# Weight transfers and later scores held to the written order, |w| of the later weights on VectorE, the gate's middle tap and edges on ACT and GpSimd: one core, attention, gated MLP and convolution

## The chip, the cores and the metric

The kernel runs on one core of one Trainium2 chip. The metric is the device time of one execution in microseconds. The kernel before takes 615.66 us, the median of three runs (614.83 to 617.19).

## The reference

Four batches of 576 rows, 8 heads of 64, width 512. All inputs and outputs are float32, except that the kernel gets the four large weights as 64-bit words and narrows them itself.

```python
# attention, causal window of 128 rows, a bias by distance
s = q @ k.T / 8 + bias
p = softmax(where(mask, s, -1e9));  x = p @ v
# first layer: a gated MLP whose gate mixes the rows
h = gelu(x @ w_in);  u, v = split(h)
v = (v - mean) / sqrt(var + 1e-6) * g_ln
x = x + (u * (w_sg @ v + b_sg)) @ w_out
# second layer: 3-tap convolution along the rows as a gate
h = relu(x @ w_in2)
c = cw[0]*h[t-1] + cw[1]*h[t] + cw[2]*h[t+1]
out = (h * sigmoid(c)) @ w_out2
```

## The kernel before, in words

Float32 products are made of three products of a high and a low part, so each operand is split into "hi" (a rounding copy) and "lo" (a subtraction) ahead of TensorE. In the trace `psv`, `psu`, `pss` and `pso` are the PSUM tiles of the first layer's four products (steps V, U, G and W), `psg` that of the second layer (g2, the step D, makes h and the gate; g3, the step F, makes the output), `sc`, `pT` and `o` the scores, the transposed weights and the output of the attention. q and k are loaded by steps L, V tiles by M, scores are C, their exponentials E, their norm N.

Batch 0's attention stands at the start. Then batch b's V, U, G and W are laid between the attention of batch b+1, for three rounds, while the sixteen pieces of each of the second layer's weights are narrowed and written back to a scratch in DRAM (`w2d`, two transfers for each piece, hi and lo). Stage 2 (from about 332 us) makes batch 3's V, U, G and W, and loads w_in2 back into SBUF (`w<-w2d`, 8 transfers of 512 KB); stage 3 runs D and F of the four batches.

A weight piece is narrowed by `narrowed` (L246): a transfer into a staging tile, |w| (L255 on ACT or L257 on VectorE, chosen by booked costs), a clamp (L259), three operations on bits (L260 to L262). For w_in (pieces i0.0 to i1.3, 512 KB each, five staging buffers) and w_out, `split` then makes hi and lo. For the second layer, `w2_piece` (L298) writes hi on GpSimd over the staging tile itself (L303), lo over the |w| tile, and sends both to DRAM; there are two staging buffers, so the next-but-one piece's transfer waits for that write to land.

`_steps` writes out the order of the steps by hand. The instructions are then ordered by the framework's scheduler; `tc.keep_in_program_order(ins)` pins an instruction behind the one that was traced before it on the same engine. Before the change only the |w| on ACT and the clamp are pinned. All transfers of these stages are issued from SP's queue, in order. The choice of an engine (`ON`, a list per operation) goes by booked costs.

In g2 the middle tap is `scaled(cc, ..., ON["tap"])` (its operation is L198), the outer taps are L645 and L646 on VectorE, the last 64 or first 64 columns of h times its gate are the "edge", split into `gr` hi (L181) and lo (L187).

## Time and profile before

| | |
|---|---|
| median of three runs | 615.66 us |
| profiled execution | 614.43 us, its span 612.4 us |
| mean granted TensorE clock | 0.975 of full speed |
| TensorE busy (PE) | 562.5 us, 92% of the span |
| VectorE (DVE) / ACT / GpSimd (POOL) | 399.1 / 244.7 / 256.2 us |

The page gives each engine's busy time. PE is the engine to follow: what the kernel can save is its idle time, some 50 us in all, and the time in which its clock was granted at less than full speed. A busy share says little of the others. DVE's 65% is made of stretches in which it is full and others in which it waits, and the same holds for SP's queue, whose transfers start in the order in which they are issued.

### The profile page before, as it was taken

To read this page: it belongs to the slowest core of one execution; us is meant where nothing else is said; L and a number is where in the kernel's file an instruction comes from. 1 tells how busy PE (TensorE), PEld (TensorE's weight loads), DVE (VectorE), ACT (ScalarE), POOL (GpSimd) and SP (SyncE) were. 2 spreads that over 40 slices of the span, in tenths; PEclk is the share of its full clock that TensorE was granted. 3 is DMA by queue.
4 is the path that set the end of the run, shared out by engine and by line. 5 is a ranking of instruction groups with operands and counts; after the bars stand their busy time and mean duration, and the time that the engine had idled before them with its cause. 6 is when DMAs were issued, how large, how long until landed. Compare 5 with 4: busy or idle time off the path is not lost.

```text
span 612.4 us, 10380 instructions
## 1 busy us (share of the span) xinstructions
PE 562.5 (92%) x3704; PEld 480.4 (78%) x3704; DVE 399.1 (65%) x981; ACT 244.7 (40%) x626; POOL 256.2 (42%) x403
## 2 busy tenths in 40 slices
PE   6499959799998999999999997996899999999998
PEld 3366649588778888779798897886789898998887
DVE  3877957454585885586875855759996666556600
ACT  4764107863026744127733211115445333334311
POOL 0763655962142741245542634425664223322310
PEclk9799969899999899999999999997999999999999
DMA  8733402141324144424235847662200100000011
GB/s 303 278 119 102 144 2 89 40 137 33 105 100 129 45 156 128 134 58 125 66 110 152 313 136 227 206 222 78 78 17 35 55 17 18 36 18 17 18 51 52
DMA packets 44851, 63.55 MB, mean 104 GB/s; under 512 B 4352, under 2 KB 27392, under 8 KB 44800
## 3 DMA queue, kind: packets, MB, share of 16 engines
q1 hardware_dynamic: 44656, 62.60, 31.5%
q8 instruction: 29, 0.48, 0.3%
q10 hardware_dynamic: 144, 0.29, 0.1%
q14 instruction: 22, 0.18, 0.1%
HBM read 45.05 MB, written 17.83 MB: 103 GB/s over the span
## 4 chain that ended last, share of the span: by engine, by line
PE 56%; DVE 17%; DMA 12%; POOL 5%; issue 4%; ACT 4%; SPq 0%; POOLq 0%; DVEq 0%; ACTq 0%
PE psg L168 26%; PE pso L168 6%; PE o L168 6%; PE sc L168 4%; PE psv L168 4%; PE pss L168 4%; DMA w<-in_w_in_dram 4%; PE pT L402 3%; DMA w<-in_w_out_dram 3%; DVE t L360 3%; DMA w2d<-w 3%; ACT t L142 2%; PE psu L168 2%; DVE wa L261 1%; DVE wa L259 1%
## 5 line engine op out<-in xcount | busy, mean ns | idle before, releaser
L168 PE MATMUL psg<-x2g,w 128*128 128x288 f32 x768 | 108.3, 297 | 0.1
L168 PEld LDWEIGHTS psg<-x2g,w 128*128 128x128 f32 x768 | 105.8, 190 | 2.1 <-ACT hb L641 0.3
L168 PE MATMUL psg<-wout,gh 128*128 128x512 f32 (+1 forms) x272 | 82.4, 387 | 8.0 <-ACT gh L177 8.0
L142 ACT ACTIVATE t<-t,mx 128x256 f32<-128x256 f32 (+1 forms) x144 | 67.2, 469 | 23.2 <-DVE mx L360 23.1
L168 PE MATMUL pss<-wsg,vn 128*128 128x256 f32 (+1 forms) x448 | 66.4, 304 | 7.0 <-DVE t L529 7.0
L168 PEld LDWEIGHTS pss<-wsg,vn 128*128 128x128 f32 x448 | 61.9, 194 | 8.7 <-DVE t L529 8.1
L168 PE MATMUL sc<-k,q 64*128 64x256 f32 (+2 forms) x320 | 53.7, 408 | 11.8 <-DMA q<-in_q_dram 6.3
L168 PEld LDWEIGHTS psg<-wout,gh 128*128 128x128 f32 x272 | 49.8, 190 | 18.8 <-ACT gh L177 8.9
L168 PE MATMUL psu<-xh,win 128*128 128x256 f32 (+1 forms) x256 | 54.9, 307 | 8.7 <-POOL win L181 5.9
L360 DVE CUSTOM_DVE_ANT_0 t<-sc,tab 128x256 f32<-128x256 f32 (+2 forms) x144 | 47.8, 379 | 17.3 <-PE sc L168 17.2
L168 PE MATMUL pso<-gh,wo 128*128 128x256 f32 (+1 forms) x256 | 55.0, 308 | 4.1 <-DVE t L529 1.6
L198 POOL TENSOR_SCALAR t<-t,r 128x256 f32<-128x256 f32 (+2 forms) x105 | 51.3, 506 | 14.0 <-DVE r L387 6.7
L181 POOL TENSOR_SCALAR gr<-gg 128x64 fp32r<-128x64 f32 x30 | 16.4, 547 | 94.8 <-DVE gg L187 94.8
L168 PEld LDWEIGHTS sc<-k,q 64*128 64x128 f32 (+1 forms) x320 | 30.2, 198 | 32.4 <-issue 13.5
L168 PE MATMUL psg<-wout,gl 128*128 128x512 f32 (+1 forms) x136 | 52.4, 385 | 1.3 <-POOL gl L187 1.3
L168 PEld LDWEIGHTS psu<-xh,win 128*128 128x128 f32 x256 | 42.7, 196 | 11.5 <-POOL win L181 6.4
L168 PE MATMUL psv<-win,xh 128*128 128x512 f32 (+1 forms) x160 | 49.9, 397 | 0.0
L168 PEld LDWEIGHTS pso<-gh,wo 128*128 128x128 f32 x256 | 40.6, 190 | 9.0 <-DVE x L187 2.1
L187 POOL TENSOR_TENSOR gl<-gg,gh 128x512 fp32r<-128x512 f32 x32 | 43.9, 1375 | 8.2 <-ACT gh L177 8.2
L168 PE MATMUL o<-ph,V 128*64 128x128 f32 (+2 forms) x448 | 41.3, 301 | 3.1 <-ACT ph L177 2.9
L198 DVE TENSOR_SCALAR cc<-hb,cw 128x576 f32<-128x576 f32 x30 | 20.3, 680 | 30.3 <-ACT hb L641 30.3
L181 POOL TENSOR_SCALAR w<-wa 128x256 fp32r<-128x256 f32 x32 | 13.7, 428 | 62.4 <-DVE wa L262 45.6
(78 smaller groups left out, 1053.6 us busy)
## 6 DMA issues: line engine op xcount, KB each, us to landing
w<-in_w_out_dram SPq DMA_DIRECT2D x24, 256.0 KB, 2.8
V<-in_v_dram SPq DMA_DIRECT2D x16, 320.0 KB, 3.5
k<-in_k_dram SPq DMA_DIRECT2D x16, 288.0 KB, 3.1
x2s<-x2d SPq DMA_DIRECT2D x16, 288.0 KB, 2.8
q<-in_q_dram SPq DMA_DIRECT2D x15, 288.0 KB, 3.5
w<-in_w_in_dram SPq DMA_DIRECT2D x8, 512.0 KB, 7.8
w<-in_w_in_dram SPq DMA_DIRECT2D x16, 256.0 KB, 2.9
w2d<-w SPq DMA_DIRECT2D x32, 128.0 KB, 2.0
```

Of the source, the lines that this page charges most:

```text
L142: ins = nc.scalar.activation(*args, **kw)
L168: nc.tensor.matmul(out, lhsT, rhs, start=start, stop=stop, **kw)
L181: nc.gpsimd.tensor_scalar(dst, src, 1.0, 1.0, op0=ALU.mult, op1=ALU.mult)
L187: (nc.vector if eng == "dve" else nc.gpsimd).tensor_tensor(dst, a, b, op=op)
L198: e.tensor_scalar(dst, src, col, 1.0, op0=ALU.mult, op1=ALU.mult)
L259: tc.keep_in_program_order(clamp.tensor_scalar(f(a), f(a), W_LOW, W_HIGH, op0=ALU.max, op1=ALU.min))
L261: nc.vector.scalar_tensor_tensor(a, high, 0xC0000000, a, op0=ALU.bitwise_and, op1=ALU.bitwise_or)
L360: nc.vector.tensor_tensor_reduce(e, banks[4 if i == 4 else (j, i // 2)][:, o : o + nk], tab[:, m, tc], scale=-SCALE, scalar=3e38, op0=ALU. ...
L402: nc.tensor.transpose(ps[:, n * P : (n + 1) * P], s["t"][:, c0 : c0 + P], ident)
```

## The change

Six edits. (1) In `_steps` the pieces i0.0 to i0.3 of w_in stand each in front of one of batch 0's V steps, and in the first round the scores of batch 1 stand behind the first steps of U. (2) w_in's transfers are pinned behind the transfer traced before them. (3) The first score product and one mask of each group of scores, for batches 1 to 3, are pinned. (4) For all weights except w_in (the one whose staging tag is "vn"), |w| is on VectorE alone; the choice by cost is left for w_in, and on VectorE too |w| is pinned now. (5) `w2_piece` puts hi into a tile of its own, `wh`, and in stage 2 takes |w| from the pool tag "v", so the staging buffer is free once L262 has read it. (6) "tap" may go to ACT or POOL only, "edge hi" and "edge lo" to POOL only.

```diff
--- before.py
+++ after.py
@@ -37,8 +37,8 @@
     "norm": "dve pool",
     "x hi": "act pool", "x lo": "dve", "vn hi": "pool", "vn lo": "dve",
     "gate": "pool", "g hi": "act dve pool", "g lo": "dve pool", "x2 hi": "act pool", "x2 lo": "dve",
-    "tap": "act dve pool", "glu": "dve", "a hi": "act", "a lo": "pool",
-    "edge hi": "act dve pool", "edge lo": "dve",
+    "tap": "act pool", "glu": "dve", "a hi": "act", "a lo": "pool",
+    "edge hi": "pool", "edge lo": "pool",
 }
 
 W_LOW = 2.0**-15
@@ -72,20 +72,24 @@
     put_by = [f"a{i}.{c}" for i in range(2) for c in range(16)]
     s = ["k0", "L0.0", "k2", "k1", "M0.0"] + scores(0) + loads(1) + ["i1.0"] + weigh(0) + scores(1) + loads(2) + ["i1.1"] + weigh(1)
     s += scores(2) + loads(3) + ["i1.2"] + back(0) + halves(0) + weigh(2) + scores(3) + ["i1.3"] + back(1) + halves(1) + weigh(3)
-    s += back(2) + halves(2) + back(3) + halves(3) + ["k3"] + [f"i0.{k}" for k in range(4)]
+    s += back(2) + halves(2) + back(3) + halves(3) + ["k3"]
     for b in range(B - 1):
         p = NP * (b + 1)
         V = [f"V{b}.{j}" for j in range(5)]
         U = [[f"U{b}.{half}.{m}" for m in range(4)] for half in range(2)]
         G = [[f"G{b}.{half}.{m}" for m in range(4)] for half in range(2)]
         W = [[f"W{b}.{half}.{m}" for m in range(4)] for half in range(2)]
-        uv = V[:2] + loads(p) + scores(p) + V[2:] + loads(p + 1) + scores(p + 1) + U[0] + loads(p + 2) + U[1][:1] + scores(p + 2) + U[1][1:]
+        if b == 0:
+            V = [x for k in range(4) for x in (f"i0.{k}", V[k])] + V[4:]
+            uv = V + loads(p) + U[0][:1] + scores(p) + U[0][1:] + loads(p + 1) + scores(p + 1) + loads(p + 2) + U[1][:2] + scores(p + 2) + U[1][2:]
+        else:
+            uv = V[:2] + loads(p) + scores(p) + V[2:] + loads(p + 1) + scores(p + 1) + U[0] + loads(p + 2) + U[1][:1] + scores(p + 2) + U[1][1:]
         T, A = ([f"{x}{of(p + i)}" for i in range(4)] for x in "TA")
         gw = weigh(p) + G[0] + weigh(p + 1) + G[1][:1] + loads(p + 3) + T[:1] + W[0][:1] + A[:1] + halves(p) + scores(p + 3)
         gw += weigh(p + 2) + W[0][1:2] + T[1:2] + W[0][2:] + A[1:2] + halves(p + 1) + weigh(p + 3) + G[1][1:2] + T[2:3] + G[1][2:3]
         gw += A[2:3] + halves(p + 2) + G[1][3:] + T[3:] + W[1][:1] + A[3:] + halves(p + 3) + W[1][1:]
         if b == 0:
-            s += weave(uv, [f"g{c}" for c in range(5)] + [f"o{k}.0" for k in range(4)]) + ["o0.1"] + gw[:2] + ["o1.1"] + gw[2:4] + ["o2.1"] + gw[4:6] + ["o3.1"] + gw[6:]
+            s += uv[:9] + weave(uv[9:], [f"g{c}" for c in range(5)] + [f"o{k}.0" for k in range(4)]) + ["o0.1"] + gw[:2] + ["o1.1"] + gw[2:4] + ["o2.1"] + gw[4:6] + ["o3.1"] + gw[6:]
         else:
             now = put_by[10 * b - 10 : 10 * b]
             s += weave(uv, now[:4]) + weave(gw, now[4:])
@@ -165,7 +169,7 @@
         per = 2 if lhsT.dtype == F32 else 1
         book_pe = max(width(rhs), 2 * width(lhsT) if per == 1 else width(lhsT)) * per / 2.4
         load["pe"] += book_pe
-        nc.tensor.matmul(out, lhsT, rhs, start=start, stop=stop, **kw)
+        return nc.tensor.matmul(out, lhsT, rhs, start=start, stop=stop, **kw)
 
     def copy(dst, src, psum=False, engines="act dve pool"):
         n = width(src)
@@ -240,21 +244,21 @@
     winh, winl = (w.rearrange("p (k n) -> p k n", k=NK) for w in wA)
     kept = {}
 
-    staged = []
     STAGE = dict(st=S, vn=1024, w64=512)
 
     def narrowed(src, n, pool, tag, bufs, spool, stag, sbufs):
 
         st = spool.tile([P, STAGE[stag]], U32, tag=stag, name="w64", bufs=sbufs)
-        nc.sync.dma_start(st[:, : 2 * n], src)
-        staged[:] = [st]
+        dma = nc.sync.dma_start(st[:, : 2 * n], src)
+        if stag == "vn":
+            tc.keep_in_program_order(dma)
         words = st[:, : 2 * n].rearrange("p (n w) -> p n w", w=2)
         low, high = words[:, :, 0], words[:, :, 1]
         a = pool.tile([P, 256 if tag == "wa" else 512], U32, tag=tag, name="wa", bufs=bufs)[:, :n]
-        if pick(dict(act=52 + 0.85 * n, dve=67 + 0.52 * n)) == "act":
+        if stag == "vn" and pick(dict(act=52 + 0.85 * n, dve=67 + 0.52 * n)) == "act":
             tc.keep_in_program_order(nc.scalar.activation(f(a), f(high), AF.Abs))
         else:
-            nc.vector.tensor_scalar(a, high, 0x7FFFFFFF, None, op0=ALU.bitwise_and)
+            tc.keep_in_program_order(nc.vector.tensor_scalar(a, high, 0x7FFFFFFF, None, op0=ALU.bitwise_and))
         clamp = nc.gpsimd if pick({e: c for e, c in dict(dve=67 + 0.52 * n, pool=147 + 0.93 * n).items() if e in ON["clamp"]}) == "pool" else nc.vector
         tc.keep_in_program_order(clamp.tensor_scalar(f(a), f(a), W_LOW, W_HIGH, op0=ALU.max, op1=ALU.min))
         nc.vector.tensor_scalar(a, a, 0x07FFFFFF, 3, op0=ALU.bitwise_and, op1=ALU.logical_shift_left)
@@ -299,8 +303,8 @@
 
         src = (w_in2, w_out2)[i].bitcast(U32).rearrange("p k n -> p (k n)")[:, 512 * c : 512 * (c + 1)]
         pool = p2pool[0] if p2pool else apool
-        a = narrowed(src, 256, pool, "wa", 2, pool, "w64", 2)
-        hi = staged[0][:, :256].bitcast(F32R)
+        a = narrowed(src, 256, *((mpool, "v", NV) if p2pool else (pool, "wa", 2)), pool, "w64", 2)
+        hi = pool.tile([P, 256], F32R, tag="wh", name="wh", bufs=1 if p2pool else 2)
         lo = a.bitcast(F32R)
         copy(hi, a, engines=ON["w64 hi"])
         tt(lo, a, f(hi), ALU.subtract, ON["w64 lo"])
@@ -351,16 +355,20 @@
                 banks[of] = aps.tile([P, 512], F32, tag="a", name="sc", bufs=NA)
             d = slice(j * D, (j + 1) * D)
             out = banks[of][d if i == 4 else slice(0, P), o : o + nk]
-            mm(out, s["q"][d, q0 : q0 + nq], s["k"][d, k0 : k0 + nk], start=True, stop=True)
+            ins = mm(out, s["q"][d, q0 : q0 + nq], s["k"][d, k0 : k0 + nk], start=True, stop=True)
+            if b and (j, i) == (0, 4):
+                tc.keep_in_program_order(ins)
 
         def masked(j, i):
             o, nk = BLK[i][6], BLK[i][3]
-            e, c, tc = weights(s, j, i)
+            e, c, part = weights(s, j, i)
             book("dve", 80 + nk)
-            nc.vector.tensor_tensor_reduce(
-                e, banks[4 if i == 4 else (j, i // 2)][:, o : o + nk], tab[:, m, tc],
+            ins = nc.vector.tensor_tensor_reduce(
+                e, banks[4 if i == 4 else (j, i // 2)][:, o : o + nk], tab[:, m, part],
                 scale=-SCALE, scalar=3e38, op0=ALU.add, op1=ALU.min, accum_out=s["mx"][:, c : c + 1],
             )
+            if b and (j, i) == (1, 0):
+                tc.keep_in_program_order(ins)
 
 
         for j, i in ((0, 4), (1, 0), (0, 0), (1, 1), (0, 1)):
```

On the queue of SP, at the program's start (w are pieces of weights, k, q and V the attention's inputs, gln and bsg small tables; `128x1024` is a w_in piece, `128x512` one of w_in2), before:

```order
L249 DMA w_140<-in_w_in_dram 128x1024
L249 DMA w_201<-in_w_in_dram 128x1024
L249 DMA w_262<-in_w_in_dram 128x1024
L249 DMA w_372<-in_w_in_dram 128x1024
L560 DMA gln<-in_g_ln_dram 128x4
L561 DMA bsg<-in_b_sg_dram 128x576
L249 DMA w_570<-in_w_in_dram 128x1024
L249 DMA w_1796<-in_w_in_dram 128x512
L249 DMA w_1890<-in_w_in_dram 128x512
L321 DMA k<-in_k_dram 128x576
L321 DMA q<-in_q_dram 128x576
L249 DMA w_580<-in_w_in_dram 128x1024
```

and of the change:

```order
L252 DMA w_140<-in_w_in_dram 128x1024
L568 DMA gln<-in_g_ln_dram 128x4
L569 DMA bsg<-in_b_sg_dram 128x576
L252 DMA w_1796<-in_w_in_dram 128x512
L252 DMA w_1891<-in_w_in_dram 128x512
L325 DMA k<-in_k_dram 128x576
L325 DMA q<-in_q_dram 128x576
L325 DMA k<-in_k_dram 128x576
L325 DMA q<-in_q_dram 128x576
L325 DMA k<-in_k_dram 128x576
L325 DMA q<-in_q_dram 128x576
L329 DMA V<-in_v_dram 128x5x128
```

Of w_in only the first piece is left ahead of the later heads' k and q. The second is in the next row behind these, behind the third V tile (two V buffers), which waits for a buffer that batch 0's attention frees.

On DVE, at the end of batch 1's first gate product (t is the gate taken out of `pss`, gh and gl its split, wa the |w| of a second-layer piece), before:

```order
L262 SCALAR_TENSOR_TENSOR wa<-w_3296,wa 128x256
L529 SCALAR_TENSOR_TENSOR t_3202<-pss,gln,bsg 128x256
L257 TENSOR_SCALAR wa<-w_3403 128x256
L259 TENSOR_SCALAR wa<-wa 128x256
L179 CAST gh<-t_3202 128x256
L529 SCALAR_TENSOR_TENSOR t_3224<-pss,gln,bsg 128x256
L260 TENSOR_SCALAR wa<-wa 128x256
L187 TENSOR_TENSOR gl<-t_3202,gh 128x256
L261 SCALAR_TENSOR_TENSOR wa<-w_3403,wa 128x256
```

and of the change:

```order
L266 SCALAR_TENSOR_TENSOR wa<-w_3167,wa 128x256
L537 SCALAR_TENSOR_TENSOR t_3216<-pss,gln,bsg 128x256
L183 CAST gh<-t_3216 128x256
L537 SCALAR_TENSOR_TENSOR t_3238<-pss,gln,bsg 128x256
L191 TENSOR_TENSOR gl<-t_3216,gh 128x256
L183 CAST gh<-t_3238 128x256
L394 TENSOR_SCALAR r<-sm_90 128x9
L537 SCALAR_TENSOR_TENSOR t_3260<-pss,gln,bsg 128x256
L191 TENSOR_TENSOR gl<-t_3238,gh 128x256
```

Between the first t and the second there stood the start of another piece, whose first operation reads a staging tile; in the change no piece stands between them.

On PE, in stage 2 where V of batch 3 meets the first products of the second layer (three `psg` tiles, w_3893 and w_3894, or w_3913 and w_3914, are the hi and lo of w_in2 as loaded back), before:

```order
L168 MATMUL psv<-win_99,xl 128x512
L168 MATMUL psg_4648<-x2g,w_3893 128x288 x2
L168 MATMUL psg_4689<-x2g,w_3893 128x288 x2
L168 MATMUL psg_4728<-x2g,w_3893 128x288 x2
L168 MATMUL psv<-win_99,xh 64x512
L168 MATMUL psv<-win_100,xh 64x512
```

and of the change:

```order
L172 MATMUL psv<-win_99,xl 128x512
L172 MATMUL psg_4680<-x2g,w_3913 128x288 x2
L172 MATMUL psg_4721<-x2g,w_3913 128x288 x2
L172 MATMUL psg_4760<-x2g,w_3913 128x288 x2
L172 MATMUL psg_4680<-x2g,w_3914 128x288 x2
L172 MATMUL psg_4680<-x2g,w_3913 128x288 x2
L172 MATMUL psg_4721<-x2g,w_3914 128x288 x2
L172 MATMUL psg_4721<-x2g,w_3913 128x288 x2
L172 MATMUL psg_4760<-x2g,w_3914 128x288 x2
L172 MATMUL psg_4760<-x2g,w_3913 128x288 x2
```

Before, six products on the hi tile stand behind 48 products of V and the next behind 12 more; in the change 54 of them, three of the four parts of both tiles, stand in one row behind the first 24 products of V.

## Rows read from the trace of the kernel before

**Rows 1.** Windows of the span: each engine's busy us, granted clock, DMA share, GB/s.
```profile
15.00:30.00 15.00, 6.96 (x40) 4.56 (x38) 13.44 (x54) 11.31 (x43) 11.51 (x19) 0.77 0.79 292
...
75.00:90.00 15.00, 6.26 (x27) 4.97 (x26) 10.11 (x31) 0.77 (x2) 8.31 (x11) 0.67 0.10 33
...
285.00:300.00 15.00, 12.97 (x95) 10.59 (x94) 14.20 (x38) 12.07 (x49) 9.98 (x18) 1.00 0.24 71
...
420.00:450.00 30.00, 26.34 (x166) 23.86 (x165) 29.30 (x37) 12.40 (x22) 20.54 (x19) 0.98 0.17 48
450.00:600.00 150.00, 150.00 (x849) 133.19 (x848) 86.28 (x118) 51.70 (x86) 42.47 (x48) 1.00 0.09 30
```

**Rows 2.** Waits of PE: engine, line, releaser: us in total, times, longest.
```profile
PE psg L168 <- ACT gh L177: 8.0, 3, 5.7
PE pss L168 <- DVE t L529: 7.0, 5, 3.1
```

**Rows 3.** Timeline of SP's queue, 0 to 52 us: start, us, issue, count.
```profile
5.25 2.77 SPq L249 DMA_DIRECT2D w<-in_w_in_dram  x4
...
44.27 0.56 SPq L325 DMA_DIRECT2D V<-in_v_dram  x1
```

**Rows 4.** Timeline of PE, 0 to 35 us; in brackets the idle time ahead.
```profile
21.70 4.49 PE L168 MATMUL sc<-k,q 64*64 64x192 f32 x20 [6.12 <-DMA q<-in_q_dram]
...
30.34 1.30 PE L168 MATMUL o<-ph,V 128*64 128x256 f32 x10 [2.25 <-ACT ph L177]
```

**Rows 5.** Timeline of PE, 35 to 100 us.
```profile
71.11 2.69 PE L168 MATMUL sc<-k,q 64*64 64x192 f32 x20 [0.19 <-DVE mx L360]
...
86.35 0.58 PE L168 MATMUL psu<-xh,win 128*128 128x256 f32 x1 [1.01 <-POOL win L187]
...
98.81 1.36 PE L168 MATMUL pss<-wsg,vn 128*128 128x256 f32 x10
```

**Rows 6.** Chain that ended last, 176 to 212 us: start, us, what.
```profile
190.26 3.66 DMA w2d<-w
```

**Rows 7.** Timeline of DVE, 180 to 202 us.
```profile
197.15 0.29 DVE L257 TENSOR_SCALAR wa<-w 128x256 uint32<-128x256 uint32 x1 [3.40 <-DMA w<-in_w_in_dram]
```

**Rows 8.** Timeline of PE, 160 to 400 us.
```profile
198.81 5.50 PE L168 MATMUL pss<-wsg,vn 128*128 128x256 f32 x28 [2.58 <-DVE t L529]
```

**Rows 9.** Timeline of PE, 364 to 404 us.
```profile
378.38 2.32 PE L168 MATMUL pss<-wsg,vn 128*128 128x320 f32 x14 [3.09 <-DVE t L529]
```

**Rows 10.** Timeline of ACT, 366 to 452 us.
```profile
376.05 0.43 ACT L255 ACTIVATE wa<-w 128x256 f32<-128x256 f32 x1 [3.60 <-DMA w<-in_w_out_dram]
```

**Rows 11.** Timeline of PE, 325 to 452 us.
```profile
331.99 0.63 PE L168 MATMUL psv<-win,xh 128*128 128x512 f32 x2
...
342.90 0.94 PE L168 MATMUL psg<-x2g,w 128*128 128x288 f32 x6
```

**Rows 12.** Timeline of SP's queue, 320 to 450 us.
```profile
335.98 3.21 SPq L595 DMA_DIRECT2D w<-w2d  x6
```

**Rows 13.** DMA issues, 335.9 to 339.3 us: KB each, median us to landing.
```profile
w<-w2d SPq DMA_DIRECT2D x6, 512.0 KB, 6.9
```

**Rows 14.** Groups of instructions, shapes apart: busy us, mean ns, idle before.
```profile
L168 PE MATMUL psg<-x2g,w 128*128 128x288 f32 x768 | 108.3, 297 | 0.1
...
L187 POOL TENSOR_TENSOR gl<-gg,gh 128x512 fp32r<-128x512 f32 x32 | 43.9, 1375 | 8.2 <-ACT gh L177 8.2
...
L360 DVE CUSTOM_DVE_ANT_0 t<-sc,tab 128x256 f32<-128x256 f32 x96 | 37.2, 417 | 2.6 <-PE sc L168 2.5
...
L187 DVE TENSOR_TENSOR gr<-gg,gr 128x64 fp32r<-128x64 f32 x32 | 25.4, 797 | 5.8 <-POOL gr L181 4.0
...
L198 DVE TENSOR_SCALAR cc<-hb,cw 128x576 f32<-128x576 f32 x30 | 20.3, 680 | 30.3 <-ACT hb L641 30.3
...
L181 POOL TENSOR_SCALAR gr<-gg 128x64 fp32r<-128x64 f32 x30 | 16.4, 547 | 94.8 <-DVE gg L187 94.8
...
L198 POOL TENSOR_SCALAR cc<-hb,cw 128x576 f32<-128x576 f32 x2 | 2.6, 1309 | 0.0
```

## The prediction

> **What bounds the kernel now.** I read the windows first, since the bound changes with the stage. The reader is to see that PE is full from 450 us to the end of its work (150.00 of 150 us) and nearly full in most of what is ahead, so that the kernel can win only where PE idles or runs at a reduced clock: 15 to 30 us (8.0 us idle, clock 0.77), 75 to 90 us (8.7 us, 0.67), 285 to 300 us (2.0 us) and 420 to 450 us (3.7 us) [rows 1]. Second, the waits of PE, which name who is late: ACT's gh once for 5.7 us and the gate product's t on VectorE five times [rows 2]. Third, for each of these places the timelines of PE and of the engine or queue behind it. They show that VectorE is late for two different reasons: it is full (29.30 of 30 us from 420 us) [rows 1], or it waits in order behind a weight's transfer (3.40 us at 197 us) [rows 7].
>
> **The change part by part.** The sum is made against the profiled execution: 614.43 us, 1.2 us below the median of the runs.
>
> *Start, 0 to 99 us: w_in later, scores of batch 1 later.* PE waits 6.12 us for a q [rows 4] that stands in SP's queue behind five w_in pieces, four of them issued from 5.25 us [rows 3], the fifth in the order above. The change leaves one of the five ahead of it. Four pieces of 512 KB are 2.1 MB, at the 292 GB/s of that window [rows 1] 7.2 us, so the q lands before PE asks and the 6.12 us go. What is late next is the exponentials' chain: already PE waits 2.25 us at 30 us for ACT's ph [rows 4]. I take 4 us as what the attention of batch 0 keeps. Against it, the w_in pieces now stand behind V tiles that wait for buffers freed by this attention, so that V's products must wait for the last piece of that half. Before, the second of these V tiles was issued at 44.27 us [rows 3]; behind it the last two pieces of V's half would land at 45 to 47 us and be narrowed, two on a busy VectorE, some 7 us later. I put PE's wait for them at 3 us, an estimate by the queue's order.
>
> Then U. Before, its last waits end at 86.35 us [rows 5], in a window in which VectorE is busy 10.1 of 15 us and PE 6.3, at clock 0.67 [rows 1]. The 27 masks of the moved scores, at 0.417 us for the larger shape [rows 14] some 9 us of VectorE's work, no longer stand ahead of the narrowing, so I expect the last U piece 6 to 8 us earlier. But three groups of scores that filled PE ahead of U, 2.69 us each [rows 5], 8.1 us, now have to be done behind the same piece. From 86.35 to the first gate product at 98.81 us are 12.5 us [rows 5], part of it at half clock. So 86.35 − 7 + 12.5 + 8.1 − 1.5 (clock) gives 98.5 us: as before. With the 4 − 3 us of the attention I take +1 for this stage, between −8 (the piece is no earlier, the scores come on top) and +6 (the wait for q survives as gain).
>
> *The pieces of the second layer, 100 to 332 us.* At 197 us VectorE waits 3.40 us for a piece's transfer [rows 7]; the second t of the gate product stands behind it, and PE waits 2.58 us for it [rows 8]. The chain shows why the transfer was late: it waits for the write of hi to DRAM (3.66 us) from the same staging buffer [rows 6]. With hi in its own tile the write is off that loop, and in the new order no piece stands between the first t and the second. The 2.58 us go. Behind them PE needs 5.50 us for 28 products [rows 8], where ten at 98.81 us take 1.36 us [rows 5] and 28 would 3.8, so the slow clock behind the stall gives another 1.7. One round later the same place costs 2.0 us [rows 1]; I count 1.5 of it. Sum +5.5 (3 to 6.5), as what remains late is the gate's own chain. The |w| moved to VectorE cost it 27 times 0.29 us [rows 7], 7.8 us over 300 us in which it is mostly not full, and take 27 times 0.43 us [rows 10], 11.6 us, from ACT, which PE waits for in other places: 0.
>
> *Stage 2, gate.* At 378 us PE waits 3.09 us for t [rows 9]. VectorE stands behind a |w| on ACT which waits 3.60 us for its transfer [rows 10]. With |w| in VectorE's own order and the buffer free earlier, +3 (1.5 to 4.5).
>
> *Stage 2, the row of 54 products.* In the order above, 54 psg products now follow the first 24 V products. They need three of the four parts of w_in2, hi and lo. The loads are issued from 335.98 us, six in 3.21 us [rows 12], and take 6.9 us each in the median [rows 13], since they share the engines. Before, PE reached the first psg at 342.90 us, behind 48 products of V from 331.99 us [rows 11], 0.227 us each, and had more V and U products between the groups. In the new order 24 of them are done at 331.99 + 24 × 0.227 = 337.4 us. The sixth load is issued at about 338.7 and lands at about 346 by the median; without waits PE would end the row at 337.4 + 54 × 0.141 (108.3 us over 768 [rows 14]) = 345.0. The six parts come one behind another, the last two products' groups (some 15 products, 2 us) follow the last part, and the median is of loads of which the later ones take longer, so the row ends at 348 to 351 us. That is a new wait of 3 to 6 us; I take −5, between −7 and 0 (the transfers start earlier, as SP's queue is less held up).
>
> *Gate of the second layer, 400 to 450 us.* The tap leaves VectorE (0.680 us each) and the lo edge (0.797), for GpSimd at 1.309 and, as the hi edge, about 0.547 [rows 14]. In 420 to 450 us seven steps pass, two of them with the tap on GpSimd already. VectorE goes from 29.30 to about 29.3 − 5 × 0.68 − 7 × 0.80 = 20.3, GpSimd from 20.54 [rows 1] to 20.5 + 5 × 1.31 + 7 × 0.55 = 30.9 of 30. So one full engine is exchanged for another. The idle 3.7 us go in part: +1, between −3 (GpSimd's a lo, 1.375 us [rows 14], is late for the third product) and +3.7. The 5.7 us wait for gh at 418 us [rows 2] hangs on x2's transfer behind the last write of stage 2; I leave it.
>
> The Trainium skill weighs here (GPSIMD Engine Reference, section 4.1): operations with one input run at roughly line rate on GpSimd, those with two about twice as slow. The tap has one input. By that rule GpSimd would take it for about VectorE's price, its load would stay under 28 us and this term would be +3.7, the whole about 3 us better. The two taps in the trace say otherwise (1.309 against 0.680 us [rows 14]), so the rows decide.
>
> *450 us to the end.* PE is full, GpSimd busy 42.5 of 150 us [rows 1]. 23 more taps and edges, about 43 us, still fit. 0.
>
> Sum: +1 + 5.5 + 3 − 5 + 1 = +5.5 us. 614.4 − 5.5 = 608.9 profiled, 615.7 − 5.5 = 610.2 for the median. Forecast 610.
>
> **Rivals.** *A: what is won is given back at once.* The 54 products wait 7 us and GpSimd bounds the gate (−3). Then 1 + 5.5 + 3 − 7 − 3 = −0.5, about 616; in the milder half 613. For it: the six loads that count share the engines, and none is issued before the last piece of w_in2 has been written to DRAM. Against it: GpSimd's 1.3 us is measured beside a full VectorE.
>
> *B: slower, by w_in.* The place is U of batch 0. If its last piece is not ready earlier than 86.35 us, since its transfer now waits for buffers, the 8.1 us of scores come on top at the full: −8 instead of +1, so 610 + 9 = 619. It decides where the last U piece is ready later than about 83 us. For it: eight transfers with waits ahead of them in place of free ones at 5 us. Against it: DMA was busy only 10% from 75 to 90 us [rows 1], so the transfers themselves are quick, and VectorE has 9 us less to do ahead.
>
> *C: more.* The start keeps its 6 us, the 54 products find the loads ready, and the gate wins its 3.7: 6 + 5.5 + 3 − 2 + 3 = 15.5, about 600. For it: clocks that fell behind each stall [rows 1] stay up. Against it: the scores have to be done somewhere.
>
> That the change does not do what it says (the scheduler undoes it) is excluded by the order shown.
>
> **How the numbers follow.** Forecast (606 to 612.5) 0.40, A 0.23, B 0.20, C 0.17. The likeliest is 610. What a measurement can tell from no change is about 0.5%, 3.1 us: 612.6 to 618.7. Faster is the forecast and C, 0.57; same is A, 0.23; slower B, 0.20. The range runs from C's 600 to just behind B's 619: 600 to 620, with half of C and two fifths of B outside.
>
> **What would show it.** Right: no wait of PE for q at 21 us; pss of batch 0 starting at 97 to 100 us; no wait of PE above 1 us for t at 198, 286 and 378 us, no long waits of SP ahead of a weight's transfer for `w2d<-w`; new waits of PE psg for `w<-w2d` of 4 to 6 us between 337 and 351; GpSimd near full in the 30 us behind the first F. Wrong: pss of batch 0 behind 103 us (B), psg waits for the loads under 1 us (C), or PE idle for POOL's gl or cc in 420 to 450 us by more than 4 us (A).

## The result: slower by 1.3%

The changed kernel takes 624.10 us (median of four runs, 623.10 to 625.37) against 615.76 for the kernel before in the same runs: a ratio of 1.0129, 95% interval 1.0105 to 1.0153. Forecast was 610, the range 600 to 620. The profiled execution takes 625.01 us, its span 623.2, at a mean granted clock of 0.959 (0.975 before).

Windows of the changed kernel (busy us of PE, PE's loads, DVE, ACT, POOL, then granted clock, DMA share, GB/s), to be laid beside [rows 1]:

```profile
15.00:30.00 15.00, 10.64 (x54) 6.89 (x56) 9.36 (x47) 11.65 (x44) 10.18 (x22) 0.77 0.25 85
...
75.00:90.00 15.00, 6.80 (x22) 4.69 (x24) 10.09 (x13) 1.07 (x2) 8.08 (x10) 0.50 0.13 37
...
285.00:300.00 15.00, 15.00 (x118) 13.98 (x117) 9.83 (x26) 14.03 (x54) 7.50 (x14) 1.00 0.12 35
...
420.00:450.00 30.00, 23.18 (x139) 21.23 (x137) 25.89 (x25) 15.61 (x25) 26.83 (x25) 0.89 0.29 87
450.00:600.00 150.00, 148.78 (x852) 133.20 (x853) 71.27 (x79) 54.98 (x90) 84.06 (x106) 0.99 0.08 29
```

PE does more in 15 to 30 us, for the wait for q is gone, and VectorE less (9.4 against 13.4 us), for it has no w_in to narrow yet. At 75 to 90 us PE stands as it did, and its granted clock is 0.50 in place of 0.67; of the clock's two levels 1.00 is the higher (2.4 GHz) and 0.50 the lower (1.2 GHz). 285 to 300 us is full now. In 420 to 450 us it is GpSimd that is nearly full. PE's 3 us less there are no loss by themselves, for the program runs 10 us later: a wait for gh that ended ahead of this window before, at 418 us, now falls into it:

```profile
425.69 1.59 PE L172 MATMUL psg<-wout,gh 128*128 128x512 f32 x4 [3.22 <-ACT gh L181]
```

PE's waits in the changed kernel, beside [rows 2]:

```profile
PE o L172 <- ACT ph L181: 7.8, 3, 3.3
PE psu L172 <- POOL win L185: 7.3, 2, 4.8
...
PE psg L172 <- POOL gl L191: 4.8, 4, 2.2
PE psg L172 <- DMA w<-w2d: 3.3, 1, 3.3
...
PE pss L172 <- DVE t L537: 2.0, 2, 1.2
```

The gate product's wait for t fell from 7.0 to 2.0 us, that for gh from 8.0 to 3.2. New is the load of w_in2 (3.3 us). The wait for gl grew from 1.3 to 4.8 us, for ph from 2.9 to 7.8, for w_in's hi from 5.9 to 7.3.

Where the time went is read best at fixed places of PE's program, from the starts of its groups in the two timelines. Start of batch 0's first gate product: 98.81 [rows 5] and 108.72 us, 9.9 lost. From there to V of batch 3: 233.2 us before (it starts at 331.99 [rows 11]), 227.0 in the change (at 335.69), 6.2 won. From there to the end of batch 3's last `pso`: 70.8 and 77.2 us, 6.4 lost. From there to the end of PE's last product: 206.6 and 207.1 us. Together 10.5 of the two spans' 10.8.

The first of these, in PE's timeline of the changed kernel (idle time ahead in brackets):

```profile
16.68 6.54 PE L172 MATMUL sc<-k,q 64*64 64x192 f32 x20 [3.10 <-DVE r L395]
27.96 1.30 PE L172 MATMUL o<-ph,V 128*64 128x256 f32 x10 [2.68 <-ACT ph L181]
...
54.02 3.51 PE L172 MATMUL o<-ph,V 128*64 128x256 f32 x28 [3.28 <-ACT ph L181]
...
87.90 0.58 PE L172 MATMUL psu<-xh,win 128*128 128x256 f32 x1 [1.01 <-POOL win L191]
...
88.63 4.21 PE L172 MATMUL sc<-k,q 64*64 64x192 f32 x20
...
96.08 2.72 PE L172 MATMUL sc<-k,q 64*64 64x192 f32 x20
...
102.44 2.72 PE L172 MATMUL sc<-k,q 64*64 64x192 f32 x20
...
108.72 1.48 PE L172 MATMUL pss<-wsg,vn 128*128 128x256 f32 x11
```

q came in time, but DVE and ACT take most of it back at once. U's last wait ends at 87.90 us, not earlier than the 86.35 of before [rows 5], and behind it stand three groups of scores, 9.7 us, the first at a granted clock of 0.62 (4.21 us in place of 2.72). SP's queue shows when w_in was asked for; the last of the three issues from 58.15 us went out at 76.5:

```profile
32.91 0.62 SPq L252 DMA_DIRECT2D w<-in_w_in_dram  x1
...
44.91 1.57 SPq L252 DMA_DIRECT2D w<-in_w_in_dram  x3
...
58.15 18.67 SPq L252 DMA_DIRECT2D w<-in_w_in_dram  x3
```

SP's waits from 25 to 110 us name the reason: the staging buffer is read last by L266.

```profile
SPq L252 <- DVE wa L266: 17.2, 2, 16.8
```

There are five such buffers, but in kernel.py they bear the tag "vn" (L285), which is also that of V's five normed rows (L467). L266 frees the buffer at 76.4 us when it is done with the first of the two pieces asked for from 58.15 us, only two transfers ahead of the one that waits. So just two of the five buffers served w_in then; by the kernel's text the others held rows of V, which stay until the gate product, and with a piece in front of each V step rows and pieces alternate. This is read from the text and the trace; no run gives w_in buffers of its own.

The third place, stage 2, in PE's timeline from 330 us:

```profile
344.62 9.19 PE L172 MATMUL psg<-x2g,w 128*128 128x288 f32 x54 [3.29 <-DMA w<-w2d]
...
368.45 0.79 PE L172 MATMUL psu<-xh,win 128*128 128x256 f32 x2 [2.61 <-ACT v L146]
```

The row of 54 products waits 3.29 us and runs 9.19 us instead of the 7.6 that 54 times 0.141 us would be, at a granted clock of 0.82. U waits 2.61 us for ACT's gelu of v. Before, groups of five to seven psg products stood between V's end and U and between U's groups, and U had no such wait; now the first 72 of them stand ahead of V's last tile.

The gate's instructions in the change (shapes apart: busy us, mean ns, idle before), beside [rows 14]:

```profile
L191 POOL TENSOR_TENSOR gl<-gg,gh 128x512 fp32r<-128x512 f32 x32 | 45.9, 1435 | 2.1 <-ACT gh L181 2.1
...
L202 POOL TENSOR_SCALAR cc<-hb,cw 128x576 f32<-128x576 f32 x32 | 30.1, 943 | 34.4 <-ACT hb L649 34.4
...
L191 POOL TENSOR_TENSOR gr<-gg,gr 128x64 fp32r<-128x64 f32 x32 | 18.2, 570 | 2.0
...
L185 POOL TENSOR_SCALAR gr<-gg 128x64 fp32r<-128x64 f32 x32 | 16.1, 504 | 22.6 <-DVE gg L191 22.6
```

### The profile page after: what moved, and what is told of

Read it like the earlier page. It is cut to its first block, busy times and chain, and to the rows that moved or that the text cites. A ratio compares the mean times of both kernels' runs of the same rounds, so it can differ in the third digit from the quotient of the medians.

```text
span 623.2 us, 10338 instructions
## 1 busy us (share of the span) xinstructions
PE 566.7 (91%) x3704; PEld 487.5 (78%) x3704; DVE 385.0 (62%) x948; ACT 236.0 (38%) x598; POOL 300.1 (48%) x464
## 4 chain that ended last, share of the span: by engine, by line
PE 58%; POOL 10%; DVE 8%; DMA 6%; issue 3%; ACT 2%; SPq 1%; POOLq 0%; ACTq 0%; DVEq 0%
PE psg L172 26%; PE psu L172 7%; PE pso L172 6%; PE sc L172 5%; PE psv L172 4%; PE o L172 4%; PE pss L172 4%; PE pT L410 3%; POOL gl L191 2%; DMA w<-in_w_out_dram 2%; DMA x2s<-x2d 2%; POOL cc L202 1%; ACT t L146 1%; DVE t L202 1%; POOL t L202 1%
## 5 line engine op out<-in xcount | busy, mean ns | idle before, releaser
L172 PEld LDWEIGHTS psg<-x2g,w 128*128 128x128 f32 x768 | 109.0, 196 | 5.9 <-issue 3.7
L172 PE MATMUL psg<-x2g,w 128*128 128x288 f32 x768 | 110.3, 303 | 3.4 <-DMA w<-w2d 3.3
L172 PE MATMUL psu<-xh,win 128*128 128x256 f32 (+1 forms) x256 | 56.8, 314 | 13.3 <-POOL win L185 7.3
L172 PE MATMUL pss<-wsg,vn 128*128 128x256 f32 (+1 forms) x448 | 64.4, 299 | 2.0 <-DVE t L537 2.0
L172 PEld LDWEIGHTS pss<-wsg,vn 128*128 128x128 f32 x448 | 60.2, 190 | 3.2 <-DVE t L537 2.8
L202 POOL TENSOR_SCALAR t<-t,r 128x256 f32<-128x256 f32 (+2 forms) x105 | 53.0, 523 | 13.3 <-DVE r L395 13.2
L653 DVE SCALAR_TENSOR_TENSOR cc<-hb,cw,cc 128x576 f32<-128x576 f32 x32 | 28.4, 892 | 49.1 <-POOL cc L202 49.1
L191 DVE TENSOR_TENSOR gg<-cc,hb 128x576 f32<-128x576 f32 x32 | 35.5, 1108 | 21.1 <-ACT cc L146 21.0
L191 POOL TENSOR_TENSOR gl<-gg,gh 128x512 fp32r<-128x512 f32 x32 | 45.9, 1435 | 2.1 <-ACT gh L181 2.1
L202 POOL TENSOR_SCALAR cc<-hb,cw 128x576 f32<-128x576 f32 x32 | 30.1, 943 | 34.4 <-ACT hb L649 34.4
```

The source lines that it names most:

```text
L172: return nc.tensor.matmul(out, lhsT, rhs, start=start, stop=stop, **kw)
L191: (nc.vector if eng == "dve" else nc.gpsimd).tensor_tensor(dst, a, b, op=op)
L202: e.tensor_scalar(dst, src, col, 1.0, op0=ALU.mult, op1=ALU.mult)
L653: nc.vector.scalar_tensor_tensor(cc, h[:, 0:S], cw[:, 0, c : c + 1], cc, op0=ALU.mult, op1=ALU.add)
```

## The experiments

Each ratio is to the kernel before, in three rounds on the same chip (95% interval). One of PE's marks, the start of batch 0's first gate product, is given as "gate" (98.81 before).

| run | us | ratio | gate |
|---|---|---|---|
| start alone | 627.68 | 1.0159 (1.0091 to 1.0227) | 107.46 |
| second layer's pieces alone | 612.75 | 0.9931 (0.9896 to 0.9967) | 99.18 |
| tap and edges alone | 620.81 | 1.0053 (1.0020 to 1.0085) | 99.15 |
| change without the start | 618.34 | 1.0021 (0.9989 to 1.0052) | 99.53 |
| scores late, with pins | 621.76 | 1.0071 (1.0045 to 1.0097) | 104.27 |
| w_in late | 619.58 | 1.0048 (1.0028 to 1.0068) | 104.00 |
| pieces, stage 2 as before | 611.87 | 0.9910 (0.9880 to 0.9941) | 100.94 |
| \|w\| on VectorE and pinned | 610.75 | 0.9918 (0.9894 to 0.9942) | 100.61 |
| score pins alone | 622.15 | 1.0089 (1.0066 to 1.0112) | 101.51 |
| \|w\| pinned, engines as before | 613.45 | 0.9956 (0.9933 to 0.9979) | 99.60 |
| change without score pins | 624.52 | 1.0129 (1.0106 to 1.0152) | 108.86 |
| \|w\| and an earlier q | 614.16 | 0.9955 (0.9935 to 0.9976) | 102.82 |
| change, all \|w\| on VectorE | 624.78 | 1.0146 (1.0089 to 1.0203) | 114.60 |
| \|w\| and score pins | 613.80 | 0.9963 (0.9943 to 0.9982) | 102.47 |
| tap alone | 619.41 | 1.0047 (1.0030 to 1.0065) | 100.39 |
| \|w\| and edges | 613.39 | 0.9944 (0.9919 to 0.9968) | 99.27 |
| \|w\| on VectorE, not pinned | 647.91 | 1.0506 (1.0483 to 1.0529) | 121.53 |

### The change in its parts

Start alone: edits 1 to 3 on the kernel before.

```diff
+            V = [x for k in range(4) for x in (f"i0.{k}", V[k])] + V[4:]
+            uv = V + loads(p) + U[0][:1] + scores(p) + U[0][1:] + ...
...
+        if stag == "vn":
+            tc.keep_in_program_order(dma)
...
+            if b and (j, i) == (0, 4):
+                tc.keep_in_program_order(ins)
...
+            if b and (j, i) == (1, 0):
+                tc.keep_in_program_order(ins)
```

> The kernel before with the start's part of the change alone: w_in's pieces and the scores of batch 1 in the new written order, w_in's transfers pinned, the score groups pinned. Theory (the start is the largest loss): batch 0's first gate product starts at about 108.7 us as in the changed kernel, 9.9 us later than before, and at least 7 of them reach the end: 623 to 627 us. Rival (the lag is worked off later, where TensorE waited for weights before): the lag at 109 us is the same but the end is at 616 to 619 us.

Pieces alone: edits 4 and 5.

```diff
+        if stag == "vn" and pick(dict(act=52 + 0.85 * n, dve=67 + 0.52 * n)) == "act":
...
+            tc.keep_in_program_order(nc.vector.tensor_scalar(a, high, 0x7FFFFFFF, None, op0=ALU.bitwise_and))
...
+        a = narrowed(src, 256, *((mpool, "v", NV) if p2pool else (pool, "wa", 2)), pool, "w64", 2)
+        hi = pool.tile([P, 256], F32R, tag="wh", name="wh", bufs=1 if p2pool else 2)
```

> The kernel before with the second layer's pieces alone: |w| on VectorE, hi in its own tile. Theory (gain in the rounds, loss in stage 2): the waits for the gate's t at 198 and 286 us go, so batch 3's V starts about 6 us earlier (325 to 327 us), but the row of 54 psg products costs 6 us again: 614 to 618 us. Rival (the row of 54 costs nothing where it is reached in time): 608 to 611 us.

Tap and edges alone: edit 6.

```diff
+    "tap": "act pool", "glu": "dve", "a hi": "act", "a lo": "pool",
+    "edge hi": "pool", "edge lo": "pool",
```

> The kernel before with the gate's middle tap and edges off VectorE alone. Theory (GpSimd becomes the bound of the gate and the output product waits for its lo part): 617 to 620 us, PE waits for GpSimd's gl or tap of 3 us or more from 400 us on. Rival (one engine for another, no change): 614.5 to 616.5 us. Third (VectorE was the bound, GpSimd keeps up): 611 to 613 us.

The changed kernel with edits 1 to 3 undone:

```diff
-            V = [x for k in range(4) for x in (f"i0.{k}", V[k])] + V[4:]
...
-        if stag == "vn":
-            tc.keep_in_program_order(dma)
...
-            if b and (j, i) == (0, 4):
-                tc.keep_in_program_order(ins)
...
-            if b and (j, i) == (1, 0):
-                tc.keep_in_program_order(ins)
```

> The changed kernel with the start's part undone (order of the steps, both pins). Theory (terms add: start +10, rounds -6, stage 2 +6, gate +3): 617 to 620 us, batch 0's gate product at 98.8 us as before. Rival (the start's lag is worked off anyway, the rest is the loss): 622 to 624 us. Third (the start is the whole loss and the rest gains what was forecast): 608 to 613 us.

The start alone costs 1.59%, the pieces win 0.69%, the gate costs 0.53%: 1.43% in sum, where the change measures 1.29%, inside the intervals. The start is the loss; its lag of 9 us at the gate is not worked off. The pieces bring 0.69%, where the theory had nothing left and its rival more; without the start the change stands at 1.0021, from which no difference to the kernel before can be told.

### What of the start costs

The later scores of edit 1 with the pins of edit 3, w_in as before:

```diff
+        if b == 0:
+            uv = V + loads(p) + U[0][:1] + scores(p) + U[0][1:] + loads(p + 1) + scores(p + 1) + ...
...
+            if b and (j, i) == (0, 4):
+                tc.keep_in_program_order(ins)
...
+            if b and (j, i) == (1, 0):
+                tc.keep_in_program_order(ins)
```

> The kernel before with batch 1's scores behind U's first products, and the score groups pinned, but w_in's transfers where they were. Theory (the scores are the loss: three groups of 2.7 us of products now stand behind the last piece of U, which is ready no earlier than before): first gate product at 105 to 108 us, 621 to 625 us. Rival (with w_in early, VectorE is free of masks and narrows U's last piece 6 to 8 us sooner, which pays for them): gate product at 98 to 101 us, 614 to 618 us.

Edit 2 alone:

```diff
+        if stag == "vn":
+            tc.keep_in_program_order(dma)
```

> The kernel before with w_in's transfers pinned to the written order, so that they stand behind the later heads' k and q and behind V tiles, and nothing else. Theory (late transfers cost only what V and U wait for them, since the scores fill TensorE meanwhile): first gate product at 100 to 104 us, 617 to 621 us. Rival (the late transfers are the whole loss): 624 to 628 us, gate product at 107 us or later. Third (the wait for q at 21 us is gained): 610 to 614 us.

Edit 3 alone:

```diff
+            if b and (j, i) == (0, 4):
+                tc.keep_in_program_order(ins)
...
+            if b and (j, i) == (1, 0):
+                tc.keep_in_program_order(ins)
```

> The kernel before with the pins on the first score product and one mask of each group of scores of batches 1 to 3, nothing else: scores stand in whole groups of 10 pairs again instead of in pieces between V and U. Theory (the pins are the third part of the start's loss, and it falls in the later rounds): first gate product within 1 us of 98.8, then 3 us or more lost from V of batch 1 to V of batch 3: 618 to 622 us. Rival (the pins cost nothing, the late scores and late w_in are all): 615 to 617 us.

The changed kernel without these four lines:

```diff
-            if b and (j, i) == (0, 4):
-                tc.keep_in_program_order(ins)
...
-            if b and (j, i) == (1, 0):
-                tc.keep_in_program_order(ins)
```

> The changed kernel without the pins on scores and masks. Theory (pins and late scores belong together: without the pins the scheduler fills V with two thirds of the scores again): 5 us or more below the changed kernel, 616 to 620 us. Rival (late w_in and the gate make the loss): 621 to 625 us.

Late w_in alone costs 0.48% and puts the gate 5.2 us later, as the theory said within a microsecond. The end of U's last wait, one trace each, shows the two parts separately: 86.35 us before [rows 5], 83.10 with the later scores and w_in where it was, 90.60 with late w_in and the scores where they were, 87.90 with both in the change.

```profile
83.10 0.58 PE L171 MATMUL psu<-xh,win 128*128 128x256 f32 x1 [1.01 <-POOL win L190]
```

```profile
90.60 0.58 PE L168 MATMUL psu<-xh,win 128*128 128x256 f32 x1 [1.64 <-POOL win L187]
```

So the masks that are out of the way bring U's last piece forward by 3.3 us, and late w_in puts it back by 4.3.

Late scores with pins cost 0.71%, but the pins without late scores 0.89%: so the late scores, which the prediction took for the danger, add nothing at the end that can be measured, though they move the gate from 101.5 to 104.3 us. The pins cost in the later rounds, as expected, and the reason is in PE's waits, first of the run with the pins alone:

```profile
PE pss L168 <- DVE t L533: 11.3, 5, 3.8
```

and in VectorE's timeline of that run from 192 us:

```profile
196.22 0.47 DVE L533 SCALAR_TENSOR_TENSOR t<-pss,gln,bsg 128x256 f32<-128x256 f32 x1
200.36 0.29 DVE L257 TENSOR_SCALAR wa<-w 128x256 uint32<-128x256 uint32 x1 [3.67 <-DMA w<-in_w_in_dram]
...
201.76 0.48 DVE L533 SCALAR_TENSOR_TENSOR t<-pss,gln,bsg 128x256 f32<-128x256 f32 x1
```

A weight piece that waits for its transfer stands between two t, as in [rows 7]. In the changed kernel the pins make no difference (1.0129 with and without), so this theory fell there, and the gate stays at 108.9 us even with most scores ahead of U: then the last w_in transfer goes out at 83.7 us, and U's last wait ends only at 95.9. So the scores cost the same ahead of U's last piece or behind it. The late w_in that was tried by itself does not explain the rest: it costs 0.48%, with all its pieces asked for by 53.7 us, where this run is 1.1% above the change without the start. The four runs in which the pieces stand between the V steps have their gate at 107.5 to 114.6 us; of the others only the one with |w| unpinned comes later than 104.3. No run has this order of the pieces without the rest of the start, so that it makes the difference is likely, but not shown.

The changed kernel with |w| of w_in on VectorE too:

```diff
-        if stag == "vn" and pick(dict(act=52 + 0.85 * n, dve=67 + 0.52 * n)) == "act":
+        if False:
```

> The changed kernel with |w| of w_in on VectorE too. Theory (ACT's |w| of the fifth w_in piece stands behind the gelu of V, its staging buffer comes free late and the last piece's transfer with it): the wait of SP's queue of 16.8 us ahead of the last w_in transfer goes below 8 us, the last piece of U is ready at 84 us or earlier, first gate product at 105 us or earlier, 3 us or more below the changed kernel: 617 to 621 us. Rival (VectorE's masks and narrowing together set the time of the first gate product, in any order): gate product at 107 to 110 us, 622 to 626 us.

The theory fell; the rival has the time, but the gate moves to 114.6 us, which neither said, and the wait of SP for a staging buffer stays:

```profile
SPq L252 <- DVE wa L266: 23.0, 2, 16.5
```

So ACT's |w| is not what holds the buffer. The pieces of V's half, which are asked for at 37 and 48 us in this run (33 and 45 in the change), occupy buffers until they are narrowed, and V waits 5.3 us for them. More buffers, or w_in buffers apart from V's rows, were not tried. Whether VectorE's total work or the chain of buffers sets 108.7 us stays open.

Edit 4, w_in's transfers pinned, and its pieces set between the loads of head pairs 2 and 3, some of them later:

```diff
+    s = ... + scores(1) + ["L0.2", "i1.1", "i1.2", "M0.2"] + weigh(1)
+    s += scores(2) + ["L0.3", "i1.3", "i0.0", "M0.3"] + back(0) + ...
...
+        if stag == "vn":
+            tc.keep_in_program_order(dma)
...
+        if stag == "vn" and pick(dict(act=52 + 0.85 * n, dve=67 + 0.52 * n)) == "act":
```

> The kernel before with |w| of the later weights on VectorE and pinned, and w_in's transfers pinned to a written order in which heads 2 and 3's k and q stand ahead of w_in's second to fifth piece, but no w_in piece stands behind a V tile. Theory (the wait for q is worth something if w_in does not pay for it): PE's 6 us wait for q gone, first gate product at 96 to 98 us, 607 to 610 us. Rival (the exponentials' chain takes what the q gives): 610 to 612 us. Third (U waits for its pieces longer): 613 to 616 us.

On top of edit 4, an earlier q is no gain, more likely a loss (0.9955 against 0.9918, the intervals just meet). The 6 us wait for q is gone, and PE's timeline shows what comes in its place:

```profile
16.65 6.14 PE L168 MATMUL sc<-k,q 64*64 64x192 f32 x20 [3.13 <-DVE r L389]
...
31.84 2.40 PE L168 MATMUL o<-ph,V 128*64 128x256 f32 x10 [4.02 <-ACT ph L177]
```

And U's last wait ends at 89.30 us, against 87.15 with edit 4 alone.

### What of the pieces wins

Edits 4 and 5, but hi over the staging tile in stage 2:

```diff
+        hi = staged[0][:, :256].bitcast(F32R) if p2pool else pool.tile([P, 256], F32R, tag="wh", name="wh", bufs=2)
```

> The kernel before with the second layer's pieces of the change (|w| on VectorE, pinned; hi in its own tile), but in stage 2 hi over the staging tile as before, by which the psg products of stage 2 stand in groups of 5 to 7 between V, U and the gate products again. Theory (the row of 54 costs 4 us by its waits for w_in2 and the clock behind them): batch 3's V at 325 to 326 us, no wait of psg for w_in2 above 0.5 us, 606 to 610 us. Rival (what the row costs is paid in another place, since stage 2 waits for its pieces again): 611 to 614 us.

Edit 4 alone, hi over the staging tile as before:

```diff
+        if stag == "vn" and pick(dict(act=52 + 0.85 * n, dve=67 + 0.52 * n)) == "act":
...
+            tc.keep_in_program_order(nc.vector.tensor_scalar(a, high, 0x7FFFFFFF, None, op0=ALU.bitwise_and))
```

> The kernel before with |w| of the later weights on VectorE and pinned, nothing else: hi still over the staging tile. Theory (VectorE's order is what took the piece from between the first and second t, so the waits at 198 and 286 us go with this edit alone): as the run with hi in its own tile in stage 1, within 2 us, batch 3's V at 325 to 327 us. Rival (the write to DRAM that holds the staging tile is the cause): batch 3's V at 329 us or later, 612 to 616 us.

The pin without the choice of the engine:

```diff
+            tc.keep_in_program_order(nc.vector.tensor_scalar(a, high, 0x7FFFFFFF, None, op0=ALU.bitwise_and))
```

> The kernel before with |w| pinned where it is on VectorE, but ACT still taken for two thirds of the pieces by cost. Theory (the gain comes from VectorE's own |w|, which lets the scheduler's order put no piece between two t): 615 to 617 us, the waits at 198 and 286 us as before. Rival (the pin is what gains): 609 to 613 us.

The choice without the pin:

```diff
+        if stag == "vn" and pick(dict(act=52 + 0.85 * n, dve=67 + 0.52 * n)) == "act":
```

> The kernel before with |w| of the later weights on VectorE for all pieces, but not pinned. Theory (engine and pin each give half: the pin keeps a piece's first operation from being put ahead of its transfer, the engine spares ACT's hop): 612 to 614.5 us. Rival (the engine without the pin gives nothing or loses, since the scheduler is free to put |w| between two t again): 615 to 620 us, waits of PE for t above 1 us at 190 to 300 us.

The pin on scores and masks on top of edit 4:

```diff
+            if b and (j, i) == (0, 4):
+                tc.keep_in_program_order(ins)
...
+            if b and (j, i) == (1, 0):
+                tc.keep_in_program_order(ins)
```

> The kernel before with |w| of the later weights on VectorE and pinned, and the pins on scores and masks. Theory (the pins alone cost 5 us since weight pieces come to stand between two t; with |w| pinned they can't): no wait of PE for t above 1 us at the second and third gate, 611 to 614 us. Rival (the pins cost their 5 us by themselves): 615 to 618 us.

Edit 4 alone brings the whole gain, 0.82%; the tile of hi's own adds nothing to it, and the rival that said the write to DRAM does it all fell. The start of V of batch 3 in the traces says the same: 331.99 us before, 327.25 with edit 4, 325.43 with both edits, 329.59 with the pin alone. What edit 5 brings without edit 4 was not run. VectorE's timeline of the run with edit 4 alone, from 188 us, beside [rows 7]:

```profile
193.47 0.48 DVE L529 SCALAR_TENSOR_TENSOR t<-pss,gln,bsg 128x256 f32<-128x256 f32 x1 [2.34 <-PE pss L168]
194.87 0.29 DVE L179 CAST gh<-t 128x256 fp32r<-128x256 f32 x1 [0.92 <-POOL t L187]
195.31 0.48 DVE L529 SCALAR_TENSOR_TENSOR t<-pss,gln,bsg 128x256 f32<-128x256 f32 x1
```

No piece between the two t, and VectorE waits for PE, not PE for it. The pin alone does the same at this place and wins 0.44%; the engine without the pin loses 5.06%, which no theory had. Of the 35.6 us between the spans of the two traces without and with the pin (646.2 and 610.6 us) 20.9 are lost by the first gate product (121.53 against 100.61). VectorE is busy 79.1 of the first 100 us there, 74.7 with the pin, and SP's queue stands 15.1 us of the first 70 in front of writes to DRAM whose hi GpSimd has not made yet:

```profile
SPq L308 <- POOL w L181: 15.1, 4, 8.2
```

Later PE waits longest for t:

```profile
135.13 8.26 PE L168 MATMUL pss<-wsg,vn 128*128 128x256 f32 x42 [10.08 <-DVE t L529]
```

VectorE's timeline has nothing but pieces from 121 to 134 us, and then

```profile
134.60 0.87 DVE L529 SCALAR_TENSOR_TENSOR t<-pss,gln,bsg 128x256 f32<-128x256 f32 x2
```

So unpinned, the scheduler puts pieces ahead of work that PE waits for, and in order that work stands behind all of them, the waits for their transfers included (29.1 us of VectorE in the whole run, 18.3 with the pin).

On top of edit 4 the score pins cost some 0.45% (0.9963 against 0.9918), half of what they cost alone, and PE has no wait above 0.5 us for t in the two rounds, where the pins alone leave 8.0 us. So about half of their cost most likely came from the pieces between two t, though the intervals are too wide to say how much; the other half is not explained (the gate is 1.9 us later, 102.47 against 100.61).

With the pieces' edits but stage 2 as before (the run above with hi over the staging tile there), the psg products stand in small groups again; PE has no wait for w_in2 and takes 72.3 us from V to the end of `pso`, where the pieces alone with the row of 54 take 75.2. Their ratios (0.9910 and 0.9931) don't tell the two apart, so the theory's 606 to 610 us was not reached: 3 us in the trace, not shown at the end.

### What of the gate costs

```diff
+    "tap": "act pool", "glu": "dve", "a hi": "act", "a lo": "pool",
```

> The kernel before with the middle tap off VectorE, the edges as before. Theory (the tap at 1.3 us is what GpSimd can't carry): 617.5 to 620 us, like the run with taps and edges. Rival (the edges are, since they stand ahead of the lo part on GpSimd): 615 to 617 us.

Edges alone, on top of edit 4:

```diff
+    "edge hi": "pool", "edge lo": "pool",
```

> The best version so far (|w| of the later weights on VectorE and pinned) with the edges' hi and lo on GpSimd, taps as before. Theory (VectorE is full around 420 to 450 us and loses 0.8 us per step, GpSimd has room without the taps): 608 to 610 us. Rival (GpSimd's lo part comes later by the edges): 612 to 615 us.

The tap alone costs 0.47%, all but the whole of the 0.53%; the edges on the best version cost 0.26% more or nothing (0.9944, interval to 0.9919, against 0.9918). PE's waits from 395 to 460 us with tap and edges on GpSimd, where the kernel before has 1.3 us for gl:

```profile
PE psg L168 <- POOL gl L187: 4.7, 3, 2.2
```

GpSimd is busy 14.92 of 15 us there from 435 to 450 us, ACT 6.36, and VectorE 13.79:

```profile
435.00:450.00 15.00, 11.36 (x60) 9.80 (x59) 13.79 (x13) 6.36 (x11) 14.92 (x15) 0.84 0.29 80
```

From the end of batch 3's last `pso` to PE's last product are 206.6 us before, 209.9 with the tap alone and 211.1 with tap and edges. Of the 3.3 us for the tap alone the wait for gl explains only some 1 us (2.2 against 1.3); there the granted clock is 0.83 from 430 to 460 us, where it is 1.00 before.

The version to keep is edit 4 alone: 610.75 us, faster than both kernels.

## Why the prediction was wrong, step by step

*Start, taken at +1, between −8 and +6: it cost 9.9 us.* This is the step that failed, and in it the term "86.35 − 7". U's last piece came at 87.90 us, not 79. I had put the masks that VectorE no longer has ahead of U at 6 to 8 us, and they are worth 3.3 (83.10 against 86.35); the late w_in, which that term put at nothing, costs 4.3 (90.60). VectorE now stands idle earlier, 9.36 us of work in place of 13.44 in 15 to 30 us, and eight transfers follow one another's narrowing through a ring of five buffers, of which V's rows take their share. From U's last wait to the gate product are 20.8 us instead of the 19.1 of the sum, as the three groups of scores take 9.65 us, not 8.1. Rival B named the place, the price (8.1 us of scores) and the point from which it decides (83 us), and had a chance of 0.20; its 619 falls short of 624 because it took all other terms from the forecast, stage 2 among them. The 6.12 us for q were read rightly as gone, and what is late next as well: ph, and r on VectorE; of the 4 us 3.25 were there when V began (34.13 against 37.38 us), and they were lost behind it. The runs add what the prediction had not: the late w_in costs by itself, the late scores next to nothing on top of the pins, and the pins, which it put at nothing, cost 0.89% alone and some 0.45% where no piece stands between two t.

*The pieces, +5.5: 6.2 us in the trace.* Right in size, and right that no piece stands between the t any more; the other half of the reason, the write to DRAM and the tile of its own, adds nothing beside edit 4; alone it was not run.

*Stage 2's gate, +3, and the row of 54, −5, together −2: −6.4.* The second step that failed. The wait for t at 378 us went. The row's new wait of 3.3 us is at the lower end of what was foreseen; missed were the slow run behind it (9.19 against 7.6 us, clock 0.82) and U's 2.61 us for ACT. PE is idle 8.9 us in this stage, against 5.3 before; the rest of the 6.4, some 2.7 us, is slower products.

*The gate of the second layer, +1, between −3 and +3.7: about −3* (0.53% alone; in the change's own trace the last stage lost 0.5 us only, with PE's wait for gh at its start down from the 5.7 us of [rows 2] to 3.2). "One full engine is exchanged for another" was right, and the forecast should have stood at its lower end: GpSimd's a lo (`gl` in the trace) is late for the third product, as the bound said, though its wait is a part of the loss only. The tap on GpSimd takes 0.943 us in the mean of 32, not the 1.309 of the two; nearer to VectorE's 0.680 than the rows of before let one think, though not at it, so the rule of the Trainium skill (GPSIMD Engine Reference, section 4.1: one input, about line rate) errs less than I held, and the load was still too much beside the rest.

*450 us to the end, 0:* PE 148.78 of 150 us; the 1.2 us missing are waits of the gate for gl, which fall into this window because the program runs 10 us later.

The sum: 625.0 profiled against the 608.9 of the forecast is 16.1 us: 10.9 by the start, 4.4 by stage 2, 1.5 by the last stage, less 0.7 by the pieces.

## What to carry to other kernels

A transfer's first reader is a wait put into an engine's queue. Where a scheduler may place it freely it can stand ahead of anything, so look in the order for what stands between two steps of the critical chain, and pin the reader, not the work beside it: the same instruction on the same engine was worth −0.8% pinned and +5% not. A wait that vanishes at the start of a chain is worth what the next engine leaves of it, and late loads make an engine idle early that is missed later; count the busy time of that engine up to the place, not only what is taken out ahead of it.

## What the runs showed that I had not expected

The clock alone can move the same order of PE's products by more than 4 us. Up to batch 1's attention the run with tap and edges alone has the same products in the same order as the kernel before, and waits that agree within 0.1 us, yet in its PE timeline

```profile
120.38 3.31 PE L168 MATMUL sc<-k,q 64*64 64x192 f32 x12
...
140.20 4.38 PE L168 MATMUL pss<-wsg,vn 128*128 128x320 f32 x28
```

stands where the kernel before has

```profile
119.01 1.86 PE L168 MATMUL sc<-k,q 64*64 64x192 f32 x12
...
135.45 4.37 PE L168 MATMUL pss<-wsg,vn 128*128 128x320 f32 x28
```

4.75 us lie between the two, of which 0.34 were there at the first gate product (99.15 against 98.81). The windows show the granted clock, 0.74 there and 1.00 before:

```profile
120.00:135.00 15.00, 14.65 (x92) 10.31 (x90) 10.00 (x33) 8.52 (x28) 8.67 (x17) 0.74 0.31 99
```

```profile
120.00:135.00 15.00, 14.60 (x128) 11.46 (x126) 9.06 (x35) 10.55 (x33) 11.69 (x22) 1.00 0.34 108
```

Behind the same small waits it came back some 10 us later. Marks of a single profile can therefore carry such an error, and the ratios of several rounds decide.
